# Attention and token mixer on one Trainium2 core: sixteen weight transfers move from SyncE's queue to ScalarE's

## Chip, cores and metric

The kernel runs on one core of a Trainium2 chip. The time is the device time of one execution in microseconds (us), given as the median of several runs. A profiled execution has a time of its own; its span, from the first to the last instruction, is a little shorter. The engines are PE (matmul; PEld is its weight load), DVE (VectorE), ACT (ScalarE), POOL (GpSimd) and SP (SyncE, which here only issues transfers).

## What is computed

The reference is block-causal attention over 8 batches, 8 heads, 576 positions and a head size of 64, followed by a low-rank token mixer and a feed-forward layer with a residual:

```python
scores = scale * np.matmul(q, k.transpose(0, 1, 3, 2))
scores = np.where(block_i >= block_j, scores, -1000000000.0)
attn = softmax(scores)
x = np.matmul(attn, v)          # heads joined: (8, 576, 512)
h = x.transpose(0, 2, 1) @ U @ V
u = x + h.transpose(0, 2, 1)
out = u + np.maximum(u @ w_ch1, 0.0) @ w_ch2    # 512 -> 2048 -> 512
```

q, k and v are 32-bit floats; U, V, w_ch1 and w_ch2 are 64-bit floats.

## The kernel before

**Work.** There are 64 heads, done one after the other. A head's scores, maxima, exponentials, sums, normalised rows, transposes and products with v come from `softmax`, `normalise`, `transpose` and `apply_v`. Heads 0 to 11 multiply q and k as plain 32-bit floats straight out of the buffer `raw`, of which there are two, so that head h uses the buffer of head h-2; `split_qk` (L881) fetches them (L886) and scales k on ACT (L902). After every second head `mix` (L1121) applies the token mixer to that pair of heads; after eight heads a batch's input of the feed-forward layer is complete.

**Feed-forward.** `ffn_chunk` (L431) takes 288 tokens and the first half (1024 of 2048) of the hidden units: L465 multiplies with w_ch1, L488 with w_ch2. Each operand is split into a high and a low part, and three products are added up. The two chunks of batch 0 run in two turns, the first with four of the eight blocks of 128 hidden units, the second with the others. The second half of the hidden units follows at the end, in `block_products` (L659). The feed-forward matmuls of the first half have a late rank (1e6 and up) on PE: they fill the holes that the heads leave.

**Weights of the first half.** `load_w1` and `load_w2` bring them in sixteen transfers of 128 rows x 512 doubles (512 KB): four of w_ch1 (ranks 3000 to 4500), four of w_ch2 (6100 to 7600), four of w_ch1 (9000 to 12000) and four of w_ch2 (13000 to 16000). Each goes through `split64` (L316): a fetch into `st`, one of two staging buffers; ACT takes the absolute value of the upper words (L353); DVE builds 32-bit floats from the two words in four passes (L331, L332, L337, L345); ACT writes the high part (L360), and POOL the rest (L361). `st` is free again after L345. The second half's sixteen transfers (`whole` set) use the same two buffers from about 660 us on. U and V go through `split64` first, at the start.

**Order.** Nothing is scheduled at run time. Every step is a task of the class `Plan` (L138) with an engine, an estimated duration, a rank (the smaller, the earlier), the buffers it reads and writes, and `after`, a further time until its result counts as there (transfers: `DL`, 3000 ns). `issue` (L165) runs a model of the engines: whenever one is free in the model, the ready task with the smallest rank is written out on it. The instruction streams that result are fixed, and on the chip each engine works through its own in that order, waiting for semaphores. A head h has ranks of about 1000h; its fetch of q and k has 1000(h-1) - 900. In the model a transfer of the weights keeps SP busy for max(630, 2.85 x 512) = 1459 ns.

**SP's queue before.** All transfers are issued by SP: q and k (L886), v (L925), the mixer's results to DRAM (L1173, L1178) and back (L440), the weights (L372, L387), the outputs (L499).

Of the kernel before, what the change touches and what calls it, by code (L numbers as in the profile page):

```python
# [16 lines left out]
P = 128  # L17
# [25 lines left out]
CW = 512  # L43
# [10 lines left out]
NEAR, DL = 130, 3000  # L54
# [83 lines left out]
class Plan:  # L138
# [8 lines left out]
    def add(self, engine, ns, prio, fn, reads=(), writes=(), hold=(), after=0, port=False):  # L147

        n = len(self.tasks)
        deps = set()  # L150
        for b in reads:
            deps.update(b.writers)
            b.readers.append(n)
        for b in hold:
            deps.update(b.readers, b.writers)
        for b in writes:
            deps.update(b.readers, b.writers)
            b.writers, b.readers = [n], []
        deps.discard(n)
        slots = {b for b in (*reads, *writes) if b.pool is not None}  # L160
        for b in slots:
            b.users += 1
        self.tasks.append((engine, ns, prio, fn, deps, after, slots, port or engine == "POOL"))
# [76 lines left out]
def _act(n, sbuf=False):  # L240
    return (93 if sbuf else 52) + 0.833 * n


def _dve(n):
    return 69 + 1.042 * n
# [9 lines left out]
def attention_then_mixer(  # L255
# [10 lines left out]
    nc = tc.nc  # L266
# [8 lines left out]
    add = plan.add  # L275

    def f32(ap):
        return ap.bitcast(F32)
# [29 lines left out]
    def take(r, name):  # L308
        n = used[name] = used.get(name, -1) + 1
        return r[n % len(r)]  # L310
# [2 lines left out]
    st_r = ring(fp, 2, [P, CW, 2], I32, "st")  # L313
    z_r = ring(fp, 2, [P, 2 * T], I32, "z")

    def split64(fetches, shape, hi, lo, dst, prio, gate=(), part=slice(None), whole=None):  # L316

        n = 1
        for x in shape[1:]:
            n *= x  # L320
        rows = shape[0]
        st, zt = take(st_r, "st"), take(z_r, "z")
        s, z = st[:rows, :n, :], zt[:rows, :n]
        low, upp = s[:, :, 0], s[:, :, 1]

        def fetch():
            for f in fetches:
                f(s)

        def shift():  # L330
            nc.vector.tensor_scalar(out=f32(z), in0=f32(z), scalar1=MOST, scalar2=LEAST, op0=ALU.min, op1=ALU.max)  # L331
            nc.vector.tensor_scalar(  # L332
                out=z, in0=z, scalar1=3, scalar2=0x3FFFFFFF, op0=ALU.logical_shift_left, op1=ALU.bitwise_and
            )

        def put_upper():
            nc.vector.scalar_tensor_tensor(  # L337
                out=z, in0=upp, scalar=-(1 << 30), in1=z, op0=ALU.bitwise_and, op1=ALU.bitwise_or
            )

        def put_lower():
            o, l, x = z, low, z
            if whole:
                o, l, x = whole().bitcast(I32), *(a.rearrange("p (a b) -> p a b", a=2) for a in (low, z))
            nc.vector.scalar_tensor_tensor(  # L345
                out=o, in0=l, scalar=29, in1=x, op0=ALU.logical_shift_right, op1=ALU.bitwise_or
            )

        zf = f32(z)
        if len(shape) > 2:  # L350
            zf = zf.rearrange("p (a b) -> p a b", a=shape[1])
        add("SP", max(630 * len(fetches), 2.85 * n), prio, fetch, gate, [st], after=DL)
        add("ACT", _act(n, True), prio, lambda: nc.scalar.activation(f32(z), f32(upp), AF.Abs), [st], [zt])  # L353
        add("DVE", 260 + 1.05 * n, prio, shift, [st, zt], [zt], port=True)
        add("DVE", _dve(n), prio, put_upper, [st, zt], [zt], port=True)
        if whole:
            add("DVE", _dve(n), prio, put_lower, [st, zt], dst if isinstance(dst, list) else [dst], port=True)
            return
        add("DVE", _dve(n), prio, put_lower, [st, zt], [zt], port=True)
        add("ACT", _act(n, True), prio, lambda: nc.scalar.copy(hi(), zf), [zt], [dst])  # L360
        add("POOL", 60 + 2.3 * n, prio, lambda: nc.gpsimd.tensor_sub(lo(), zf[part], f32(hi()[part])), [zt, dst], [dst])  # L361

    def load_w1(w, half, bufs, prio, parts=(0, 1), gate=(), whole=None):

        n = 0
        for o in parts:
            for k in range(KC):
                a = 2 * (half * HF + o * CW)
                at = (slice(None), k, slice(o * CW, (o + 1) * CW))
                src = w1[k * P : (k + 1) * P, a : a + 2 * CW]  # L370
                split64(
                    [lambda s, src=src: nc.sync.dma_start(out=s, in_=src.rearrange("p (n t) -> p n t", t=2))], [P, CW],  # L372
                    lambda at=at: w()["w1h"][at], lambda at=at: w()["w1l"][at],
                    bufs[o][k // 2] if whole else bufs["w1"][o][k], prio(n), gate,
                    whole=whole and (lambda o=o, k=k: whole()[:, o, k // 2, k % 2 * CW : (k % 2 + 1) * CW].rearrange(
                        "p (a b) -> p a b", a=2
                    )),
                )
                n += 1

    def load_w2(w, half, bufs, prio, gate=(), whole=None, ks=range(FC)):

        for k in ks:
            r = (half * FC + k) * P
            src = w2[r : r + P, :]
            split64(
                [lambda s, src=src: nc.sync.dma_start(out=s, in_=src.rearrange("p (n t) -> p n t", t=2))], [P, CW],  # L387
                lambda k=k: w()["w2h"][:, k, :], lambda k=k: w()["w2l"][:, k, :],
                [bufs[a][k // FH] for a in range(2)] if whole else bufs["w2"][k], prio(k), gate,
                whole=whole and (lambda k=k: whole()[:, :, k // FH, k % FH * 256 : (k % FH + 1) * 256]),  # L390
            )

    def weight_bufs():
# [109 lines left out]
    def block_products():  # L503
# [60 lines left out]

        s1 = {x: (at("w1h", n), at("w1l", n), after(end), after(end)) for n, (x, _) in enumerate(STAGES1)}
        load_w1(None, 1, whole, lambda n: L, whole=lambda: second()["whole"])
        weights(s1)

# [8 lines left out]
        for n, x in enumerate(("a11", "a12", "a22", "s2", "s3", "s1", "s4")):  # L577
            (hi, h), (lo, l) = place(2 * n), place(2 * n + 1)
            s2[x] = (hi, lo, h, l)
        load_w2(None, 1, whole, lambda k: L, whole=lambda: second()["whole"])  # L580
        weights(s2)

# [245 lines left out]
    for r in raw_r:  # L828
# [3 lines left out]
        for x, fill in ((qi, 1.0), (ki, NEG)):  # L832
            nc.gpsimd.affine_select(
                out=x[:, :, 1, :], in_=x[:, :, 1, :], pattern=[[-1, 4], [0, 64]], compare_op=ALU.not_equal,
# [13 lines left out]
    def mixing_weights(prio):  # L848


        def fetch_u(t):
# [3 lines left out]
            )  # L855

        split64(
            [fetch_u], [P, 4, R], lambda: ust[:, 0:4, 0:R], lambda: ust[:, 0:4, R : 2 * R], ust.parts[0], prio
        )
# [326 lines left out]
    mixing_weights(MP)  # L1186
    wab = weight_bufs()
    load_w1(lambda: wa, 0, wab, lambda n: WP0 + WP1 * n, (0,))
    for h in range(NH):
        pr = 1000.0 * h  # L1190
        if h + 1 < NH:
            split_qk(h + 1, max(pr - LA, 1.0))
        for g, tiles in ((1, (4, 3)), (0, (2, 1, 0))):
            for x in ((4,), (3,)) if g else ((2,), (1, 0)):
                softmax(h, x, pr + 10)
            normalise(h, tiles, pr + 10)
        for g in (1, 0):
            for part in range(2):
                transpose(h, g, part, pr + 20 + 10 * (1 - g))
            apply_v(h, g, pr + 30)  # L1200
        if h + 1 < NH:
            split_v(h + 1, pr + 1000)
        if h % 2 == 1:
            mix(h // 2, pr + 40)
        if h == min(WH, NH - 1):
            gate = Buf()
            gate.writers = [len(plan.tasks) - 1]
            load_w2(lambda: wa, 0, wab, lambda n: WPB + WP1 * n, [gate], ks=range(FH))
            load_w1(lambda: wa, 0, wab, lambda n: WP2 + WP3 * n, (1,), [gate])
            load_w2(lambda: wa, 0, wab, lambda n: WP4 + WP3 * (n - FH), [gate], ks=range(FH, FC))  # L1210
# [59 lines left out]
```

## Time and profile before

| | us |
|---|---|
| median of 3 runs | 1182.55 (1182.36 to 1183.16) |
| profiled execution | 1182.37 |
| its span | 1180.6 |
| PE busy | 1164.1 |
| DVE busy | 936.2 |
| ACT busy | 774.9 |
| POOL busy | 451.2 |
| first feed-forward matmul (L465) starts at | 99.95 |

An engine is busy while an instruction of it runs; waits, branches and the issuing of transfers do not count. Matmuls are pipelined, so a busy PE is not PE at its peak. The granted clock of PE is 1.00 throughout. In a row of a timeline stand the start, the length, the engine and line, the operation, what it writes and reads, and the count, with the idle time before it and what ended that in brackets. In a row of waits stand who waited, for whom, the total in us, how often, and the longest. "SPq" is SP's queue of transfers.

### The profile page before, as it was taken

To read this page: it belongs to the slowest core of one execution; us is meant where nothing else is said; L and a number is where in the kernel's file an instruction comes from. 1 tells how busy PE (TensorE), PEld (TensorE's weight loads), DVE (VectorE), ACT (ScalarE), POOL (GpSimd) and SP (SyncE) were. 2 spreads that over 40 slices of the span, in tenths; PEclk is the share of its full clock that TensorE was granted. 3 is DMA by queue.
4 is the path that set the end of the run, shared out by engine and by line. 5 is a ranking of instruction groups with operands and counts; after the bars stand their busy time and mean duration, and the time that the engine had idled before them with its cause. 6 is when DMAs were issued, how large, how long until landed. Compare 5 with 4: busy or idle time off the path is not lost.

```text
span 1180.6 us, 25204 instructions
## 1 busy us (share of the span) xinstructions
PE 1164.1 (99%) x8988; PEld 1131.4 (96%) x8988; DVE 936.2 (79%) x2009; ACT 774.9 (66%) x1924; POOL 451.2 (38%) x582
## 2 busy tenths in 40 slices
PE   9989999999999999999999999999999999999998
PEld 7778999999999999999999999999999999999998
DVE  6898887877887877777877587327989889889887
ACT  7888888989888888898887342114544444444443
POOL 5556876676757666766674122110000000000000
PEclk9999999999999999999999999999999999999999
DMA  4445565433433433443331434211132132132121
GB/s 142 141 153 154 160 177 140 116 115 108 114 112 110 123 105 111 114 117 110 112 94 52 142 113 145 66 52 50 61 122 71 51 121 70 53 121 62 60 81 41
DMA packets 75884, 122.69 MB, mean 104 GB/s; under 512 B 8944, under 2 KB 52976, under 8 KB 75760
## 3 DMA queue, kind: packets, MB, share of 16 engines
q1 hardware_dynamic: 75760, 121.09, 34.8%
q8 instruction: 71, 1.16, 0.4%
q14 instruction: 53, 0.43, 0.1%
HBM read 76.23 MB, written 29.49 MB: 90 GB/s over the span
## 4 chain that ended last, share of the span: by engine, by line
PE 81%; DVE 8%; ACT 7%; issue 2%; DMA 1%; SPq 0%; POOL 0%; ACTq 0%; DVEq 0%; POOLq 0%
PE bb L659 30%; PE bf L465 11%; PE bf L488 10%; PE ba L1050 7%; PE ba L1109 6%; PE bg L488 4%; PE bg L465 4%; ACT p L991 3%; DVE mx L980 2%; PE ba L967 2%; PE ba L966 2%; PE ba L1134 1%; PE bw L966 1%; PE ba L1148 1%; DVE pl L1069 1%
## 5 line engine op out<-in xcount | busy, mean ns | idle before, releaser
L1017 POOL TENSOR_SCALAR p<-p,rv 128x192 f32<-128x192 f32 (+4 forms) x320 | 171.8, 551 | 156.8 <-DVE rv L1008 85.2
L659 PE MATMUL bb<-hh,w1l 128*128 128x288 f32 x704 | 170.1, 295 | 0.0
L659 PE MATMUL bb<-hh,w1h 128*128 128x288 f32 x704 | 169.4, 295 | 0.0
L1069 DVE TENSOR_TENSOR pl<-ba,ph 128x512 fp32r<-128x512 f32 x216 | 113.7, 550 | 17.9 <-ACT ph L1027 15.7
L991 ACT ACTIVATE p<-ba,mx 128x448 f32<-128x448 f32 (+2 forms) x248 | 114.8, 466 | 16.4 <-DVE mx L980 12.8
L1050 PE MATMUL ba<-ident,p 128*128 128x128 f32 x768 | 122.8, 275 | 2.7 <-POOL p L1017 1.5
L659 PE MATMUL bb<-hl,w1h 128*128 128x288 f32 x576 | 123.0, 295 | 0.1
L659 PEld LDWEIGHTS bb<-hh,w1l 128*128 128x128 f32 x704 | 122.9, 190 | 0.0
L659 PEld LDWEIGHTS bb<-hh,w1h 128*128 128x128 f32 x704 | 121.9, 188 | 0.0
L488 PE MATMUL bf<-hh,w2h 128*128 128x288 f32 x384 | 118.8, 309 | 0.9 <-DVE hl L473 0.9
L488 PE MATMUL bf<-hl,w2h 128*128 128x288 f32 x384 | 113.5, 295 | 0.0
L488 PE MATMUL bf<-hh,w2l 128*128 128x288 f32 x384 | 112.7, 294 | 0.0
L447 POOL TENSOR_TENSOR ul<-ur,uh 128x288 fp32r<-128x288 f32 x72 | 61.5, 880 | 127.2 <-PE bf L465 80.9
L613 ACT CAST hh<-hb 128x576 fp32r<-128x576 f32 x98 | 65.9, 672 | 60.6 <-PE bb L659 59.3
L1027 ACT CAST ph<-ba 128x512 fp32r<-128x512 f32 x216 | 98.8, 491 | 9.1 <-PE ba L1050 7.8
L980 DVE TENSOR_REDUCE mx<-ba 128x1 f32<-128x448 f32 (+3 forms) x248 | 95.1, 406 | 10.1 <-PE ba L967 7.5
L1050 PEld LDWEIGHTS ba<-ident,p 128*128 128x128 f32 x768 | 89.9, 141 | 8.3 <-POOL p L1017 3.4
L659 PEld LDWEIGHTS bb<-hl,w1h 128*128 128x128 f32 x576 | 91.9, 188 | 0.4 <-DVE hl L614 0.4
L1109 PE MATMUL ba<-ph,vs 128*128 128x256 f32 (+3 forms) x432 | 89.9, 262 | 0.0
L465 PE MATMUL bf<-uh,w1l 128*128 128x288 f32 x392 | 82.1, 305 | 0.0
L913 POOL TENSOR_TENSOR k<-raw,k 64x576 fp32r<-64x576 f32 x52 | 75.1, 1444 | 2.1 <-POOL p L1017 0.5
L912 POOL TENSOR_TENSOR q<-raw,q 64x576 fp32r<-64x576 f32 x52 | 74.0, 1422 | 4.5 <-issue 2.1
(173 smaller groups left out, 3357.7 us busy)
## 6 DMA issues: line engine op xcount, KB each, us to landing
raw<-in_qk_dram SPq DMA_DIRECT2D x63, 288.0 KB, 3.9
st<-in_w_dram SPq DMA_DIRECT2D x32, 512.0 KB, 3.7
o_d<-ot SPq DMA_DIRECT2D x72, 144.0 KB, 1.8
vr<-in_v_dram SPq DMA_DIRECT2D x32, 320.0 KB, 3.7
ur<-u_d SPq DMA_DIRECT2D x64, 144.0 KB, 2.4
whole<-o_d SPq DMA_DIRECT2D x32, 288.0 KB, 3.1
out_dram<-whole SPq DMA_DIRECT2D x31, 288.0 KB, 2.2
ur<-u_d SPq DMA_DIRECT2D x30, 288.0 KB, 3.3
```

Source lines behind the costliest of these rows:

```text
L465: nc.tensor.matmul(ps[:, :T], w()[wn][:, k, fs], m[k].ap, start=(i == 0), stop=(i == len(ops) - 1))
L488: nc.tensor.matmul(ps[:, :T], w()[wn][:, f, ms], hs[f][x].ap, start=(i == 0), stop=(i == len(ops) - 1))
L659: nc.tensor.matmul(bank[:, i, :T], x()[:, w(k)], p.ap[:, k, :], start=first and n == 0, stop=last and n == len(ops) - 1)
L912: add("POOL", 1380, pr, lambda: nc.gpsimd.tensor_sub(q1[top], raw[top, 0:S], f32(q2[top])), [raw, q2], [q1])
L913: add("POOL", 1380, pr, lambda: nc.gpsimd.tensor_sub(k2[top], raw[top, S : 2 * S], f32(k1[top])), [raw, k1], [k2])
L980: lambda i=i, at=at: nc.vector.tensor_reduce(out=mx[: P if i else 64, i : i + 1], in_=view(i, at), op=ALU.max, axis=AX.XY if wide else AX. ...
L991: nc.scalar.activation(out.rearrange("p (j k) -> p j k", j=2) if wide else out, view(i, at), AF.Exp, bias=mx[:rows, i : i + 1], accum_out= ...
L1017: lambda x=x, rows=rows, i=i: nc.gpsimd.tensor_scalar(out=x, in0=x, scalar1=rv[:rows, i : i + 1], scalar2=1.0, op0=ALU.mult, op1=ALU.mult),
L1027: add("ACT", _act(n), pr, lambda: nc.scalar.copy(out(), inp()), reads, writes)
L1050: nc.tensor.transpose(out=bank[:, a : a + P], in_=pt_r[i][h % PB[i]][:, j * P : (j + 1) * P], identity=perm.ap)
L1069: "DVE", _dve(m), pr, lambda: nc.vector.tensor_sub(pl[:, low], bank[:, :m], f32(ph[:, low])), [bank, bh], [bl]
L1109: nc.tensor.matmul(bank[0 : c.stop, a:n], vs[:, j, c], x[:, _at(g, j)], start=(i == 0), stop=(i == len(ops) - 1))
```

## The change

`split64` gets an argument `queue`. For the first half's weights (`whole` not set) `load_w1` and `load_w2` now start the transfer with `nc.scalar` in place of `nc.sync`, and the task belongs to ACT, with 450 ns and a landing 1400 ns later than `DL`. The second half's transfers, U, V and all others stay with SP. No other line is touched; since the model of `Plan` sees other durations, the order of tasks on all engines is worked out anew.

```diff
-    def split64(fetches, shape, hi, lo, dst, prio, gate=(), part=slice(None), whole=None):
+    def split64(fetches, shape, hi, lo, dst, prio, gate=(), part=slice(None), whole=None, queue="SP"):
...
-        add("SP", max(630 * len(fetches), 2.85 * n), prio, fetch, gate, [st], after=DL)
+        if queue == "ACT":
+            add("ACT", 450, prio, fetch, gate, [st], after=DL + 1400)
+        else:
+            add("SP", max(630 * len(fetches), 2.85 * n), prio, fetch, gate, [st], after=DL)
...
     def load_w1(w, half, bufs, prio, parts=(0, 1), gate=(), whole=None):
 
-        n = 0
+        n, queue, start = 0, *(("SP", nc.sync) if whole else ("ACT", nc.scalar))
...
-                    [lambda s, src=src: nc.sync.dma_start(out=s, in_=src.rearrange("p (n t) -> p n t", t=2))], [P, CW],
+                    [lambda s, src=src: start.dma_start(out=s, in_=src.rearrange("p (n t) -> p n t", t=2))], [P, CW],
...
     def load_w2(w, half, bufs, prio, gate=(), whole=None, ks=range(FC)):
 
+        queue, start = ("SP", nc.sync) if whole else ("ACT", nc.scalar)
```

`load_w2` starts its transfer with `start.dma_start` in the same way, and both hand `queue=queue` to `split64`.

More of the change, by code (lines that the diff above doesn't have):

```diff
@@ L377, in load_w1 @@
                     )),
+                    queue=queue,
                 )
@@ L386, in load_w2 @@
             split64(
-                [lambda s, src=src: nc.sync.dma_start(out=s, in_=src.rearrange("p (n t) -> p n t", t=2))], [P, CW],
+                [lambda s, src=src: start.dma_start(out=s, in_=src.rearrange("p (n t) -> p n t", t=2))], [P, CW],
                 lambda k=k: w()["w2h"][:, k, :], lambda k=k: w()["w2l"][:, k, :],
@@ L390, in load_w2 @@
                 whole=whole and (lambda k=k: whole()[:, :, k // FH, k % FH * 256 : (k % FH + 1) * 256]),
+                queue=queue,
             )
```

## Prediction

> **What bounds the kernel now.** I read the page first, then the busy time by stretches, then what the matmul engine (PE) waited for, and last the rows around the sixteen transfers themselves.
>
> ```profile
> span 1180.6 us, 25204 instructions
> ...
> PE 1164.1 (99%) x8988; PEld 1131.4 (96%) x8988; DVE 936.2 (79%) x2009; ACT 774.9 (66%) x1924; POOL 451.2 (38%) x582
> ```
>
> PE is busy for 1164.1 of 1180.6 us. The change touches no matmul, so what it can win lies in the 16.5 us in which PE is idle, and in what hides in "busy" because matmuls wait for each other in the pipeline. The stretches (busy us and count of PE, of its weight loads, of DVE, ACT and POOL, then clock, DMA share and GB/s) say where the idle time lies:
>
> ```profile
> 0.00:80.00 80.00, 72.97 (x420) 59.85 (x421) 65.24 (x174) 64.81 (x180) 43.08 (x67) 1.00 0.46 143
> 80.00:160.00 80.00, 76.26 (x573) 69.80 (x572) 70.64 (x168) 67.26 (x185) 58.43 (x68) 1.00 0.59 168
> 160.00:480.00 320.00, 318.52 (x2632) 310.34 (x2631) 255.66 (x683) 281.50 (x794) 219.03 (x281) 1.00 0.41 116
> ```
>
> 7.0 + 3.7 = 10.8 us of the 16.5 us lie before 160 us; the next 320 us have 1.5 us. The weight loads on PE tell the same: 59.9 of 80 us at first, 310 of 320 later. So PE is loosely filled only until feed-forward matmuls, which can fill every hole, are there. Before that, the attention heads run as fast as their chain over PE, DVE, ACT and POOL allows, with ACT busy for 64.8 + 67.3 = 132 of 160 us (83%) and DVE for 136 (85%). The transfers that the change moves lie in just this part. What ended PE's waits before 160 us (total us, times, longest):
>
> ```profile
> PE bw L962 <- ACT raw L902: 2.3, 2, 1.2
> PE ba L1050 <- POOL p L1017: 1.5, 2, 0.8
> ...
> PE ba L1050 <- ACT p L991: 0.9, 2, 0.6
> ```
>
> ACT alone ends 3.2 us in these two rows. An ACT that falls behind is therefore felt by PE at this place, though not one for one.
>
> **What SP gives up.** Sixteen issues leave SP. Each is short, and SP stands waiting for the staging buffer before most of them (first duration ns min/median/max of the issue, then total wait us, times, longest):
>
> ```profile
> L372 SPq DMA_DIRECT2D st<-in_w_dram x16: 327/333/524, 17.7 to 685.5; - x16
> L387 SPq DMA_DIRECT2D st<-in_w_dram x16: 327/333/576, 41.0 to 735.2; - x16
> ```
> ```profile
> SPq L372 <- DVE z L345: 22.9, 8, 5.5
> SPq L387 <- DVE z L345: 21.1, 6, 6.6
> ```
>
> SP loses 16 x 0.333 = 5.3 us of issuing and up to 44.0 us of waiting. That would be a gain if something urgent were queued behind. Urgent on SP are the fetches of q and k for the head after next, which need the last score matmul that reads the buffer:
>
> ```profile
> 41.97 0.66 PE L962 MATMUL ba<-raw 128*128 128x192 f32 x4
> ...
> 44.75 1.30 PE L962 MATMUL ba<-raw 128*128 128x320 f32 x6
> ```
> ```profile
> 42.66 0.47 SPq L886 DMA_DIRECT2D raw<-in_qk_dram  x1
> ...
> 46.11 0.47 SPq L886 DMA_DIRECT2D raw<-in_qk_dram  x1
> ```
>
> The score matmuls end at 41.97 + 0.66 = 42.63 and 44.75 + 1.30 = 46.05 us, the fetches start at 42.66 and 46.11 us: 0.03 and 0.06 us later. They are bound by PE's release of the buffer, not by SP. I take 0 for SP's relief; at the outside it is worth these 0.06 us a fetch, some 0.7 us for the twelve heads whose scores read that buffer.
>
> The Trainium skill, "DMA: Bandwidth & Descriptors", section "Issuing engines are not separate DMA queues", says that issuing from several engines saves only the sequencer's issue time. The two lags agree that this time is not what anyone waits for here, so by that rule too SP's part is 0.
>
> **What a second queue may give.** One place shows a fetch that was late in landing. These rows are from SP's timeline, from the chain that ended last (start, us), and from ACT's and PE's timelines (idle before, in brackets):
>
> ```profile
> 41.01 0.33 SPq L387 DMA_DIRECT2D st<-in_w_dram  x1
> 41.39 0.90 SPq L1173 DMA_DIRECT2D u_d<-ur  x2
> ```
> ```profile
> 42.66 6.10 DMA raw<-in_qk_dram
> ```
> ```profile
> 48.78 0.68 ACT L902 ACTIVATE raw<-raw 64x576 f32<-64x576 f32 x1 [1.51 <-DMA raw<-in_qk_dram]
> ```
> ```profile
> 49.52 1.24 PE L962 MATMUL bw<-raw 128*128 128x288 f32 x4 [1.19 <-ACT raw L902]
> ```
>
> The fetch at 42.66 us came behind a weight transfer and two stores in one queue and took 6.10 us; ACT waited 1.51 us for it and PE 1.19 us. With the weight transfer in ACT's queue the fetch has only the stores ahead of it, but the same 512 KB go over the same DMA engines at about the same time. Bounds: 0 and -1.19 us. I take the middle, -0.6 us.
>
> The same page of the Trainium skill, section "Queues, rings and completion order", says that each DMA engine takes the queue rows in turn, packet by packet. By it the fetch would no longer stand behind the whole weight transfer, the full 1.19 us would be won, and the sum below would be 0.6 us lower; one queue is all that this trace has, so no row tests it.
>
> **What ACT takes on.** (1) The issues: 16 x 0.333 = 5.3 us if every one stops ACT; with the longest issue seen on SP it is 16 x 0.576 = 9.2 us; 0 if ACT's engine is still computing while its sequencer issues. The transfer's buffer is freed by the same DVE pass (L345) that frees the load's cast on ACT (L360). The cast has the smaller priority number, so the planner puts it first and the issue of the load after next behind it. The rows of DVE and of ACT there:
>
> ```profile
> 40.27 0.67 DVE L345 SCALAR_TENSOR_TENSOR z<-st,z 128x512 int32<-128x512 int32 x1
> ```
> ```profile
> 41.50 0.62 ACT L360 CAST w1h<-z 128x512 fp32r<-128x512 f32 x1
> 42.02 0.43 ACT L445 CAST uh<-ur 128x288 fp32r<-128x288 f32 x1
> ```
>
> The pass ends at 40.94 us. SP issued at 41.01 us; ACT would do it about at its cast, 41.5 to 42.1 us. A cast of 0.62 us is longer than an issue of 0.33 us, so most of it hides behind the cast, and what I charge is the overlap that is lost: the next instruction starts at 42.02 us, 0.10 us before the cast's end at 42.12 us. That is 16 x 0.10 = 1.6 us of ACT, of which I let a good third reach PE, +0.6 us. The bounds are 0 and the 9.2 us.
>
> (2) The wait for the buffer, behind which exponentials, copies and casts of the heads are queued, and so DVE, POOL and PE. The nearest rows are ACT's own waits for the same pass, before 160 us:
>
> ```profile
> ACT w1h L360 <- DVE z L345: 1.2, 2, 1.0
> ...
> ACT w2h L360 <- DVE z L345: 0.4, 1, 0.4
> ```
>
> ACT comes too early for that pass three times in sixteen, for 1.6 us in all, and that is paid already. An issue that stands behind the cast finds the pass done. I take 0; the other bound is the second rival.
>
> (3) The transfers start later, by 0.5 to 1.1 us in the example. Here is when weights are ready (POOL's last step of a load) and when PE first reads them:
>
> ```profile
> 50.06 1.26 POOL L361 TENSOR_TENSOR w1l<-z,w1h 128x512 fp32r<-128x512 f32 x1 [0.94 <-ACT w1h L360]
> ```
> ```profile
> 99.95 0.77 PE L465 MATMUL bf<-uh,w1h 128*128 128x288 f32 x4
> ```
> ```profile
> 158.62 1.28 POOL L361 TENSOR_TENSOR w2l<-z,w2h 128x512 fp32r<-128x512 f32 x1 [3.17 <-ACT w2h L360]
> ```
> ```profile
> 166.97 0.38 PE L488 MATMUL bf<-hh,w2h 128*128 128x288 f32 x1
> ```
>
> The first four are there at 51.3 us and used at 99.95 us; the sixteenth is there at 159.9 us, and the second turn that needs it starts at 166.97 us. 7.1 us of slack cover a delay of one or two; beyond 7.1 us each one would be PE's. I take 0.
>
> **The order.** The planner charges SP 1459 ns a transfer and a landing 3000 ns later; the change charges ACT 450 ns and 4400 ns. So the loads land 0.4 us later in its model and every later choice on every engine is taken anew. I see no reason for a sign and take 0, with 2.4 us to either side: the three rows of PE's waits above are six gaps with a sum of 4.7 us, 0.8 us each, so the 10.8 us are some fourteen such gaps; a new order closes some and opens others, and 2.4 us are three of them.
>
> **The sum.** Profiled execution 1182.37 us (its span of 1180.6 us and 1.8 us around it), 0.2 us below the median of 1182.55 us. 1182.37 + 0 (SP) - 0.6 (second queue) + 0.6 (issues) + 0 (waits) + 0 (later weights) + 0 (order) = 1182.4 us. Measurement tells about 0.2%, 2.4 us, from no change.
>
> **Rivals.** *The loads sink behind the heads (faster).* On SP a transfer went out as soon as its buffer was free; on ACT it must win by priority against the heads' work, which has the smaller numbers in most cases. If one or two loads slip past 100 us, DVE is relieved of their passes while the first eight heads, which the first feed-forward matmul waits for, are under way (total us, mean ns, before 160 us):
>
> ```profile
> L345 DVE SCALAR_TENSOR_TENSOR z<-st,z 128x512 int32<-128x512 int32 (+3 forms) x20 | 15.2, 762 | 0.0
> ...
> L331 DVE TENSOR_SCALAR z<-z 128x512 f32<-128x512 f32 (+3 forms) x20 | 13.6, 679 | 2.0 <-ACT z L353 1.8
> ```
>
> A load is four such passes, about 4 x 0.7 = 2.8 us of DVE at 85%. For it speaks that DVE is the busiest engine beside PE there; against it, that the planner already gives these passes the lower rank on DVE. If one load slips, the feed-forward starts up to 2.8 us sooner, with the second queue's 0.6 us about 1179.2 us. Chance 0.28.
>
> *ACT stalls at the issue (slower).* If the planner puts an issue where ACT comes to it well before the pass is done, ACT stops with all that is queued. SP's fourteen waits have a mean of 44.0 / 14 = 3.1 us. Two of these on ACT are 6.3 us; with half of that on PE, +3.1 us, and the time is 1185.5 us. It decides from two such stalls on; one, +1.6 us, is not told from no change. The cast's 1.6 us speak against it. Chance 0.18. To this side I add 0.04 for weights that come more than 7.1 us later.
>
> *The full issue cost.* If each issue stops ACT for its 0.333 us, 5.3 us of ACT cost at half about +2.7 us where I charged 0.6, so 1184.4 us: still within 2.4 us of the median, and part of my middle case. The Trainium skill, "Perfetto Trace Analysis", section "Sequencer Loop", says that engine instructions are pushed into a queue while control instructions run in the sequencer, which is the reading that makes this term small; only a trace with an issue on ACT can show it.
>
> **How the numbers follow.** The middle case has 0.50, and gives "within 0.2%"; faster has 0.28; slower 0.18 + 0.04 = 0.22. The range reaches to the faster rival's 1179.2 us and to the slower rival's 1185.5 us; what lies beyond is a part of each, together about 0.2.
>
> **What would show it.** Right: sixteen issues on ACT, each near 0.33 us and close behind a cast of the load before last; no ACT wait for L345 above 1 us; the first feed-forward matmul at 100 us, give or take 2; the q and k fetch of the seventh head landing in about 4 to 5 us; PE idle before 160 us of 9 to 13 us. Wrong: an issue that takes far longer than 0.33 us on ACT, waits of 3 us ahead of it, or a first feed-forward matmul that moved by more than 2.4 us.

## The result, and the profile after

The kernel became slower. Before: 1182.45 us (1181.61 to 1183.16). After: 1192.76 us (1192.20 to 1193.95). The ratio is 1.0089, with a 95% interval of 1.0071 to 1.0106, so 10.3 us or 0.9%. I had forecast no change (1182.4 us, up to 1185.5). The profiled execution of after took 1192.39 us. From L352 on, lines of after are 3 to 6 higher than those of before (L353 is L356, L372 is L375, L387 is L392, L465 is L471, L1050 is L1056); L331 to L345 are the same.

The page of after, span and engines:

```profile
span 1190.6 us, 25140 instructions
...
PE 1167.0 (98%) x8988; PEld 1134.8 (95%) x8988; DVE 939.7 (79%) x2009; ACT 777.8 (65%) x1924; POOL 454.2 (38%) x582
```

The span grew by 10.0 us. PE's busy time grew by only 2.9 us, its idle time by 7.1 us. The same three stretches of after as were shown of before (busy us and count of PE, PEld, DVE, ACT, POOL, then clock, DMA share and GB/s):

```profile
0.00:80.00 80.00, 74.12 (x416) 60.96 (x417) 59.24 (x169) 62.63 (x174) 40.38 (x66) 0.98 0.44 131
80.00:160.00 80.00, 72.55 (x527) 65.19 (x526) 69.16 (x158) 64.95 (x175) 57.13 (x66) 1.00 0.53 162
160.00:480.00 320.00, 314.26 (x2591) 307.19 (x2590) 250.86 (x662) 272.64 (x765) 214.05 (x271) 0.99 0.41 116
```

Look at the counts rather than at the busy time. By 160 us PE has started 416 + 527 = 943 matmuls, where before it had started 993; by 480 us 3534, where before it was 3625. So after is 50 matmuls behind at 160 us and 91 at 480 us. In the 360 us that follow, before does 2831 matmuls, 0.127 us each:

```profile
480.00:840.00 360.00, 358.96 (x2831) 354.26 (x2830) 242.83 (x548) 206.16 (x530) 130.68 (x167) 1.00 0.33 99
```

91 x 0.127 = 11.6 us, which is the 10.0 us of the span within what a count of mixed matmuls can say. Note also that in the first 80 us PE looks busier than before (74.1 for 73.0 us) with fewer matmuls done: "busy" hides the loss, the count shows it. A part of that is the granted clock (0.98 in this row): where it fell, at 44.81 us, six matmuls of 128x320 in L1099 take 2.23 us, and the same six in before take 1.20 us.

The sixteen issues themselves look as forecast. From the view of the staging buffer `st` in after (duration ns min/median/max, first and last start us), and a stretch of ACT's timeline:

```profile
L375 ACTq DMA_DIRECT2D st<-in_w_dram x8: 334/334/381, 20.8 to 108.3; - x8
L392 ACTq DMA_DIRECT2D st<-in_w_dram x8: 334/334/356, 49.4 to 147.5; - x8
```
```profile
22.05 0.44 ACT L363 CAST v<-z 96x288 fp32r<-96x288 f32 x1
22.06 0.33 ACTq L375 DMA_DIRECT2D st<-in_w_dram  x1
22.39 0.73 ACT L997 ACTIVATE p<-bw,mx 128x576 f32<-128x576 f32 x1
```

The issue (22.06 to 22.39 us) runs under the cast, and the exponential follows at once. But the loads come much later. DVE's pass L345, which frees `st`, for the twelfth of the sixteen loads, in before and in after:

```profile
102.91 0.66 DVE L345 SCALAR_TENSOR_TENSOR z<-st,z 128x512 int32<-128x512 int32 x1
```
```profile
124.61 0.69 DVE L345 SCALAR_TENSOR_TENSOR z<-st,z 128x512 int32<-128x512 int32 x1
```

That is 21.7 us later. The first feed-forward matmul of after starts at 103.65 us, 3.7 us later than before:

```profile
103.65 0.77 PE L471 MATMUL bf<-uh,w1h 128*128 128x288 f32 x4
```

Four stretches of 5 us in after show where PE stood, with the same columns:

```profile
40.00:45.00 5.00, 3.23 (x13) 2.30 (x14) 4.16 (x11) 4.23 (x13) 3.31 (x6) 0.86 0.71 186
45.00:50.00 5.00, 5.00 (x26) 3.97 (x25) 4.13 (x9) 3.61 (x9) 1.89 (x3) 0.80 0.19 66
175.00:180.00 5.00, 3.15 (x23) 2.52 (x21) 4.92 (x9) 4.95 (x12) 4.18 (x5) 1.00 0.49 148
180.00:185.00 5.00, 4.53 (x24) 4.56 (x25) 3.07 (x10) 1.00 (x4) 2.73 (x3) 0.66 0.23 62
```

Two of these are holes (3.2 of 5 us busy). DVE and ACT are at 4.9 of 5 us in the second, so PE seems to stand there for them. The row that ends it, with its wait of 2.20 us, is a product of the token mixer:

```profile
180.47 0.58 PE L1169 MATMUL ba<-v,t 96*128 96x288 f32 x1 [2.20 <-DVE rv L1013]
```

The DVE step that it names, at 180.25 us, runs behind two long passes of a load:

```profile
176.63 1.55 DVE L331 TENSOR_SCALAR z<-z 128x512 f32<-128x512 f32 x1
178.22 1.51 DVE L332 TENSOR_SCALAR z<-z 128x512 int32<-128x512 int32 x1
```

This load is not one of the sixteen, whose last L345 ends at 163.70 us. It is the first of the second half, which SP fetched already at 155.84 us; the "about 660 us" given ahead of the prediction holds for its last pass, not for its transfer. In before the same two passes took 0.68 and 0.53 us. Why they last so long here was not followed.

In or just behind each hole the granted clock falls (0.86 and 0.80; 0.66). 5 x (0.14 + 0.20) = 1.7 and 5 x 0.34 = 1.7 us are lost there by this estimate, 3.4 us of the 10 if PE bounds both.

### The profile page after: what moved, and what is told of

Same layout as the page of the kernel before. It is cut to its first block, busy times and chain, and to the rows that moved or that the text cites. A ratio compares the mean times of both kernels' runs of the same rounds, so it can differ in the third digit from the quotient of the medians.

```text
span 1190.6 us, 25140 instructions
## 1 busy us (share of the span) xinstructions
PE 1167.0 (98%) x8988; PEld 1134.8 (95%) x8988; DVE 939.7 (79%) x2009; ACT 777.8 (65%) x1924; POOL 454.2 (38%) x582
## 4 chain that ended last, share of the span: by engine, by line
PE 51%; ACT 1%; DVE 1%; issue 0%; ACTq 0%; DVEq 0%
PE bb L665 29%; PE bf L494 5%; PE bf L471 4%; PE bg L494 4%; PE bg L471 4%; PE ba L1056 1%; PE ba L1115 1%; ACT p L997 0%; PE ba L973 0%; PE ba L972 0%; PE ba L1140 0%; PE ba L1154 0%; PE bw L972 0%; PE bw L973 0%; DVE hl L620 0%
## 5 line engine op out<-in xcount | busy, mean ns | idle before, releaser
L1023 POOL TENSOR_SCALAR p<-p,rv 128x576 f32<-128x576 f32 (+4 forms) x320 | 173.0, 555 | 136.7 <-DVE rv L1014 62.4
L997 ACT ACTIVATE p<-ba,mx 128x448 f32<-128x448 f32 (+3 forms) x248 | 114.9, 466 | 16.4 <-DVE mx L986 11.9
L1056 PE MATMUL ba<-ident,p 128*128 128x128 f32 x768 | 123.2, 275 | 2.3 <-POOL p L1023 1.0
L494 PE MATMUL bf<-hh,w2h 128*128 128x288 f32 x392 | 121.7, 310 | 0.6 <-DVE ot L500 0.5
L494 PE MATMUL bf<-hl,w2h 128*128 128x288 f32 x392 | 116.3, 297 | 0.0
L494 PE MATMUL bf<-hh,w2l 128*128 128x288 f32 x392 | 115.7, 295 | 0.0
L1033 ACT CAST ph<-ba 128x512 fp32r<-128x512 f32 x216 | 100.4, 490 | 13.9 <-PE ba L1056 8.3
L1056 PEld LDWEIGHTS ba<-ident,p 128*128 128x128 f32 x768 | 90.3, 141 | 6.3 <-issue 3.4
L471 PE MATMUL bf<-uh,w1l 128*128 128x288 f32 x404 | 82.6, 302 | 0.0
L494 PEld LDWEIGHTS bf<-hh,w2h 128*128 128x128 f32 x392 | 74.5, 190 | 1.4 <-DVE ot L500 0.9
```

The lines of the kernel that those rows point to most:

```text
L471: nc.tensor.matmul(ps[:, :T], w()[wn][:, k, fs], m[k].ap, start=(i == 0), stop=(i == len(ops) - 1))
L494: nc.tensor.matmul(ps[:, :T], w()[wn][:, f, ms], hs[f][x].ap, start=(i == 0), stop=(i == len(ops) - 1))
L997: nc.scalar.activation(out.rearrange("p (j k) -> p j k", j=2) if wide else out, view(i, at), AF.Exp, bias=mx[:rows, i : i + 1], accum_out= ...
L1023: lambda x=x, rows=rows, i=i: nc.gpsimd.tensor_scalar(out=x, in0=x, scalar1=rv[:rows, i : i + 1], scalar2=1.0, op0=ALU.mult, op1=ALU.mult),
L1033: add("ACT", _act(n), pr, lambda: nc.scalar.copy(out(), inp()), reads, writes)
L1056: nc.tensor.transpose(out=bank[:, a : a + P], in_=pt_r[i][h % PB[i]][:, j * P : (j + 1) * P], identity=perm.ap)
```

## The experiments

Four explanations were set against each other. They are the letters in the expectations:

- **A, the rank.** On SP an issue goes out when its buffer is free. On ACT it must win by rank against the heads' work, so the loads slide behind the heads and come too late.
- **B, the order.** The planner's output changed, and before's order is a good one among many; any other set of numbers, with no ACT in it, would cost too.
- **C, the issue.** Issuing on ACT holds ACT up on the chip.
- **M, the model.** The loss is a hole that the planner's own model already shows: its end goes from 1141.4 us (before) to 1145.6 us (after).

Ratios are to the kernel before on the same chip, with 95% intervals; "model" is the end by the planner's model.

### The order and the issuing engine, apart

The order of the instructions is fixed when the kernel is written out, so the two halves of the change can be separated cleanly. First, before's order on all engines, with the sixteen transfers issued by ACT at the planned place:

```diff
-  [lambda s, src=src: nc.sync.dma_start(...)]
+  [lambda s, src=src: (nc.sync if whole else nc.scalar).dma_start(...)]
```

> The order of the kernel before on PE, DVE, ACT and POOL, unchanged; only the sixteen issues are taken out of SP's stream and put into ACT's, at the place that the model's time gives them. Theory B (the order that the planner writes out decides): 1181 to 1185 us. Theory C (the issue on ACT costs, by its own length and by waiting for the buffer in ACT's stream): at 16 x 0.34 us and the waits, 1186 to 1192 us. Theory A (loads that start late): the issues stand where they stood, so 1181 to 1186 us.

Second, after's order with SP as the issuer (the planner still takes the tasks for ACT's):

```diff
-  n, queue, start = 0, *(("SP", nc.sync) if whole else ("ACT", nc.scalar))
+  n, queue, start = 0, *(("SP", nc.sync) if whole else ("ACT", nc.sync))
...
-  queue, start = ("SP", nc.sync) if whole else ("ACT", nc.scalar)
+  queue, start = ("SP", nc.sync) if whole else ("ACT", nc.sync)
```

> The order of the changed kernel on PE, DVE, ACT and POOL, unchanged; only the sixteen issues are taken out of ACT's stream and put into SP's. Theory B: as slow as the changed kernel, 1189 to 1194 us. Theory C: the loss goes with the issues, 1181 to 1185 us. Theory A: SP starts a transfer as soon as the buffer is free, so the data are there earlier, but ACT's absolute value stands at its late place, so still 1187 us or more.

Measured: before's order issued by ACT takes 1183.81 us, ratio 1.0008 (0.9995 to 1.0020). After's order issued by SP takes 1190.42 us, ratio 1.0071 (1.0052 to 1.0089). The stretches, first of before's order issued by ACT, then of after's order issued by SP:

```profile
0.00:80.00 80.00, 72.41 (x413) 59.18 (x414) 63.62 (x170) 64.37 (x178) 43.10 (x67) 0.98 0.49 143
80.00:160.00 80.00, 75.81 (x564) 69.11 (x563) 70.25 (x168) 66.27 (x183) 57.26 (x68) 1.00 0.58 161
160.00:480.00 320.00, 318.50 (x2630) 310.64 (x2629) 255.99 (x684) 281.96 (x794) 219.79 (x281) 1.00 0.43 117
```
```profile
0.00:80.00 80.00, 73.40 (x417) 59.92 (x417) 59.67 (x170) 62.71 (x174) 40.50 (x66) 0.98 0.46 132
80.00:160.00 80.00, 73.34 (x535) 66.38 (x535) 70.66 (x158) 65.32 (x176) 58.13 (x66) 1.00 0.57 165
160.00:480.00 320.00, 314.27 (x2601) 307.13 (x2600) 251.64 (x667) 274.74 (x773) 215.30 (x275) 1.00 0.42 115
```

The second kernel has after's fingerprint with not one issue on ACT: DVE 59.7 us in the first 80, 952 matmuls by 160 us and 3553 by 480 us, that is 72 short of before's 3625, or 72 x 0.127 = 9.1 us. The first has before's: 3607 matmuls, 18 short, 2.3 us. The slide of the twelfth load is in the order too, here in after's order issued by SP:

```profile
124.38 0.69 DVE L345 SCALAR_TENSOR_TENSOR z<-st,z 128x512 int32<-128x512 int32 x1
```

So the order carries 1190.42 - 1182.61 = 7.8 us, some 8 of the 10.3 us. What the issue on ACT adds is 0.0008 x 1183 = 0.9 us by the one pair and (1.0089 - 1.0071) x 1183 = 2.1 us by the other; the interval of the one holds no change, and those of the other pair overlap. C is at most a small part. Nor is the granted clock the main part: the profiled execution of after's order issued by SP has one fall of its own (0.92 and 0.74 from 10 to 20 us), but another of its four runs kept a clock of 1.000 and took 1190.13 us.

### The rank

After, with its sixteen tasks put ahead of all other work of ACT:

```diff
-            add("ACT", 450, prio, fetch, gate, [st], after=DL + 1400)
+            add("ACT", 450, -1.0, fetch, gate, [st], after=DL + 1400)
```

> The changed kernel, but the sixteen issues on ACT get the rank -1, ahead of the heads' work, so that in the model ACT issues as soon as the staging buffer is free. Theory A (the loads slide: an issue on ACT waits for its turn behind the heads' work, each load starts later, and the loads' passes on DVE fall into the stretch behind 100 us): the sixteenth L345 ends near 158 us as before, not near 164, and the time comes back to 1182 to 1185 us. Theory B (any new order of the planner may cost this much, whoever issues): anything from 1178 to 1194 us, without a link to when the loads end. Theory C (ACT itself is held up on the chip by issuing): sixteen issues stay on ACT, now with more waiting for the buffer, so 1190 us or more.

Measured: 1184.63 us, 1.0015 (1.0006 to 1.0025), model 1143.6. Most of the loss is gone with ACT still issuing. The twelfth load and the first feed-forward matmul of this kernel:

```profile
106.86 1.00 DVE L345 SCALAR_TENSOR_TENSOR z<-st,z 128x512 int32<-128x512 int32 x1
```
```profile
100.43 0.77 PE L471 MATMUL bf<-uh,w1h 128*128 128x288 f32 x4
```

The loads are back (106.9 against 124.6 us), and so is the feed-forward (100.4 against 103.7 us). Two more kernels with this rank have other landing times (`after=DL + 500` and `DL + 900`), to see whether the good time belongs to the rank or to one lucky order:

> Sixteen issues on ACT with rank -1 and a model landing of 3500 ns in place of 4400. The planner's own model of the order ends 0.9 us earlier than for the kernel before (1140.5 against 1141.4 us in its own time). Theory B (a new order costs some us on the chip, whatever its model says): 1183 to 1190 us. Theory M (the loss is the hole that the model itself shows: 4.2 us later for the changed kernel): 1180 to 1183 us.

> The same with a model landing of 3900 ns; the model ends 1.1 us later than for the kernel before. Theory B: 1183 to 1190 us, and no nearer to the 3500 ns version than to others. Theory M: 1183 to 1185 us.

Measured: 1188.15 us, 1.0042 (1.0029 to 1.0054), model 1140.5; and 1186.37 us, 1.0021 (1.0012 to 1.0031), model 1142.5. And after with its old rank and only the landing put back (`after=DL`):

> The changed kernel with the old rank and a model landing of 3000 ns in place of 4400. The model ends 5.2 us later than for the kernel before, 1.0 us later than for the changed one. Theory B: 1184 to 1195 us. Theory M: 1187 to 1194 us, no faster than the changed kernel. If the 4400 ns were the cause of the loss: 1182 to 1185 us.

Measured: 1196.95 us, 1.0113 (1.0096 to 1.0130), model 1146.6: the slowest of all. So the 1400 ns do not make the loss. Much of this one is the granted clock, 0.990 to 0.993 in its four runs: in the profiled execution it is 0.83, 0.86 and 0.80 in the three stretches of 20 us from 140 to 200 us, by estimate 20 x (0.17 + 0.14 + 0.20) = 10.2 of the 14.1 us if PE bounds there. With all sixteen issues on ACT, the two orders with the heads' ranks cost 0.89 and 1.13%; with the first rank the three cost 0.15 to 0.42%. This speaks for A, but does not show it: each of the five is an order of its own, the first rank leaves a loss that differs from number to number, and it doesn't always keep the loads early. With 3500 ns the twelfth load is late with the first rank, too:

```profile
118.02 1.38 DVE L345 SCALAR_TENSOR_TENSOR z<-st,z 128x512 int32<-128x512 int32 x1
```

### Other numbers, with SP throughout

These kernels have no issue on ACT and no task of ACT's; only the numbers that the planner is given change. First SP with after's numbers (`queue` is handed on as in after, and the start is `nc.sync`):

```diff
-        add("SP", max(630 * len(fetches), 2.85 * n), prio, fetch, gate, [st], after=DL)
+        if queue == "ACT":
+            add("SP", 450, prio, fetch, gate, [st], after=DL + 1400)
+        else:
+            add("SP", max(630 * len(fetches), 2.85 * n), prio, fetch, gate, [st], after=DL)
```

> SP issues again, but the planner is given ACT's numbers for it, 450 ns and a landing 4400 ns later. Theory A: SP starts a transfer as soon as its buffer is free, so the loads end as before and the time is 1180 to 1185 us. Theory B: the model's numbers are those of the change, so the order is new, and the time may be anywhere from 1178 to 1194 us. Theory C: no issue on ACT, 1181 to 1184 us.

Then before, with the landing of the sixteen transfers 400 ns later or earlier, or with 330 ns for the issue and the landing 400 ns later:

```diff
-  add("SP", max(630 * len(fetches), 2.85 * n), ..., after=DL)
+  add("SP", max(630 * len(fetches), 2.85 * n), ..., after=DL + (400 if n == CW and not whole else 0))
```

> The kernel before, all on SP; only the model's landing time of these sixteen transfers is 3400 ns in place of 3000. That is the shift of the model's landing that the change brings, without any change of queue. Theory B: a new order on all engines, and a time that is off by several us in some direction, more likely slower, 1180 to 1192 us. Theories A and C: no issue on ACT and no waiting for a turn, 1181 to 1184 us.

> The same with 2600 ns. Theory B: again a new order, and a time off by several us, 1180 to 1192 us, with no link to the sign of the 400 ns. Theories A and C: 1181 to 1184 us.

> All on SP, and the planner is told what the chip shows for these sixteen: 330 ns of SP and a landing 3400 ns later. The model ends 1.8 us earlier than for the kernel before. Theory B: 1183 to 1190 us, for it is a new order too. Theory M: 1179 to 1182 us.

Last, two numbers that have nothing to do with the weights: the landing of q and k 200 ns later (`after=DL + 200`, L898), and POOL's normalise at 260 in place of 250 (L1016):

> The kernel before, the sixteen transfers as they were; only the model's landing time of the q and k fetches is 3200 ns in place of 3000. Theory B (any new order costs, since the order before is one of the better ones): slower by 0.1 to 0.6%, 1184 to 1190 us. If the losses belong to the weight transfers: 1181 to 1184 us.

> The kernel before; only the model's duration of the normalising step on POOL is 10 ns longer (260 + 0.85 w in place of 250 + 0.85 w). The planner's model ends 0.5 us earlier. Theory B: slower by 0.1 to 0.6%, 1184 to 1190 us. If the losses belong to the weight transfers: 1181 to 1184 us.

| kernel | time, us | ratio | interval | model, us |
|---|---|---|---|---|
| sp_with_act_numbers | 1190.36 | 1.0058 | 1.0041 to 1.0074 | 1141.0 |
| sp_landing_plus400 | 1185.50 | 1.0025 | 1.0013 to 1.0036 | 1141.0 |
| sp_landing_minus400 | 1187.77 | 1.0041 | 1.0025 to 1.0056 | 1142.9 |
| sp_cost330 | 1184.66 | 1.0016 | 1.0006 to 1.0025 | 1139.6 |
| other_raw_landing | 1183.58 | 1.0008 | 0.9998 to 1.0019 | 1143.7 |
| other_norm_cost | 1187.93 | 1.0033 | 1.0013 to 1.0052 | 1140.9 |

Not one is faster, and five of six are measurably slower, among them one that changes nothing but a normalise's estimate by 10 ns. A landing 400 ns later costs and one 400 ns earlier costs as well. This is B: before's numbers give an order that is among the good ones, and a draw of another order costs 0.1 to 0.6%. In sp_with_act_numbers the loads sink little: their L345 starts 2.6 us later than in before on the mean of the sixteen, against 11.5 us in after, and the twelfth is in its place. Still 6.9 us are lost:

```profile
103.24 0.66 DVE L345 SCALAR_TENSOR_TENSOR z<-st,z 128x512 int32<-128x512 int32 x1
```

So a loss nearly as large as that of after's order came with hardly a sinking load.

A part of these losses is the granted clock, and it is not the same part in each. Two stretches of other_norm_cost, whose seven runs all lie at 0.993 to 0.999:

```profile
60.00:80.00 20.00, 17.06 (x100) 14.18 (x100) 16.30 (x35) 13.69 (x38) 9.22 (x11) 0.91 0.41 122
80.00:100.00 20.00, 16.30 (x87) 12.80 (x86) 17.49 (x38) 16.10 (x45) 11.75 (x16) 0.91 0.46 141
```

By estimate 20 x (0.09 + 0.09) = 3.6 of its 4.7 us are lost there if PE bounds both. In the runs with a clock of 1.000 the kernel before takes 1182.3 us (median), sp_landing_plus400 1183.2 (two runs), other_raw_landing 1183.4, sp_cost330 1184.6 and sp_landing_minus400 1186.1 us (one run). So four of the orders cost 0.9 to 3.8 us without any fall of the clock, and again none is faster; the other two have no such run.

M falls as a guide: by the model sp_cost330 should have won 1.8 us and lost 1.8, other_norm_cost should have won 0.5 and lost 4.7, other_raw_landing should have lost 2.3 and shows 0.3. Of all these, only the two orders with the heads' ranks for all sixteen on ACT have a model end more than 4 us later (1145.6 and 1146.6), and they are the two slowest; there model and chip agree in sign, and the model shows less than half of the loss.

### Parts of the change

Only the first four transfers on ACT, and only the last twelve:

```diff
-  n, queue, start = 0, *(("SP", nc.sync) if whole else ("ACT", nc.scalar))
+  n, queue, start = 0, *(("SP", nc.sync) if whole or 0 not in parts else ("ACT", nc.scalar))
...
-  queue, start = ("SP", nc.sync) if whole else ("ACT", nc.scalar)
+  queue, start = "SP", nc.sync
```

For the last twelve the condition is `whole or 0 in parts`, and `load_w2` is as in after.

> Only the first four transfers (w_ch1, ranks 3000 to 4500) are issued by ACT, the other twelve by SP. Theory A: the first loads slide by 6 to 8 us as in the changed kernel and the rest catch up in part, so a part of the loss, 1183 to 1188 us. Theory B: no ordering, 1178 to 1194 us. Theory C: a quarter of the loss, about 1185 us.

> Only the last twelve transfers are issued by ACT, the first four by SP. Theory A: the first four loads run as before, the later ones slide; most of the loss, 1185 to 1192 us, with the sixteenth L345 ending behind 160 us. Theory B: 1178 to 1194 us. Theory C: three quarters of the loss, about 1190 us.

Measured: 1187.39 us, 1.0030 (1.0018 to 1.0042); and 1189.21 us, 1.0049 (1.0034 to 1.0065). Each part costs, but each is also a new order and lies within what new orders cost with SP alone. These two tell nothing apart, and I should not have expected them to.

### What an issue on ACT costs

Before's order, with each transfer as two of 64 rows, once on ACT (32 issues) and once on SP, to double the number of issues on ACT without a new order:

```diff
-  [lambda s, src=src: nc.sync.dma_start(out=s, ...)]
+  [lambda s, src=src, h=h: (nc.sync if whole else nc.scalar).dma_start(out=s[h], ...)
+      for h in ((slice(0, P),) if whole else (slice(0, 64), slice(64, P)))]
```

On SP the same halves are issued with `nc.sync` throughout.

> The same with the thirty-two issues on ACT, still in the order of the kernel before. Theory C: twice the cost of sixteen issues; if these cost 0.9 to 2 us, 2 to 4 us more than the run with halves on SP. Theory B: the order is the same, so within 2 us of it.

> The order of the kernel before on every engine; each of the sixteen transfers is issued as two of 64 rows, on SP. The control of the next run. All theories: 1181 to 1184 us.

Measured: on ACT 1191.85 us, 1.0069 (1.0054 to 1.0084); on SP 1184.17 us, 1.0007 (0.9996 to 1.0018). The halves cost nothing on SP and (1.0069 - 1.0007) x 1183 = 7.3 us on ACT, where single issues had cost 0.9. The cost is not linear in the number. ACT's timeline with the halves shows why; "x2" is two issues back to back:

```profile
43.01 0.67 ACT L353 ACTIVATE z<-st 128x512 f32<-128x512 f32 x1
43.57 1.12 ACTq L387 DMA_DIRECT2D st<-in_w_dram  x2
44.73 0.36 ACT L1027 COPY xt<-ba 64x256 f32<-64x256 f32 x1 [1.05 <-DVE ur L1168]
...
51.53 0.68 ACT L902 ACTIVATE raw<-raw 64x576 f32<-64x576 f32 x1 [0.62 <-DMA raw<-in_qk_dram]
51.53 1.19 ACTq L387 DMA_DIRECT2D st<-in_w_dram  x2
52.76 0.62 ACT L360 CAST w1h<-z 128x512 fp32r<-128x512 f32 x1 [0.55 <-issue]
```

The second pair starts together with an instruction of 0.68 us, takes 1.19 us, and ACT stands for 0.55 us. The first starts only when DVE has freed the buffer (L345 ends at 42.86 + 0.67 = 43.53 us), 0.11 us before the activation ends, and ACT stands for nearly all of its 1.12 us, 1.05 us. ACT's next instruction starts 0.04 us after each pair's end. The place of the first pair with single issues, in before's order issued by ACT, DVE's pass first:

```profile
42.27 0.67 DVE L345 SCALAR_TENSOR_TENSOR z<-st,z 128x512 int32<-128x512 int32 x1
```
```profile
42.42 0.67 ACT L353 ACTIVATE z<-st 128x512 f32<-128x512 f32 x1
42.98 0.34 ACTq L387 DMA_DIRECT2D st<-in_w_dram  x1
43.35 0.36 ACT L1027 COPY xt<-ba 64x256 f32<-64x256 f32 x1 [0.26 <-DVE ur L1168]
43.74 0.62 ACT L360 CAST w1h<-z 128x512 fp32r<-128x512 f32 x1
```

The gap of 0.26 us here carries the name of a DVE instruction, as did the 1.05 us above. It begins where the activation ends (43.09 us) and ends 0.03 us after the issue (43.32 us): the issue was the last to end, whatever the bracket says. It could not start sooner, since the buffer came free at 42.94 us: what ACT loses depends on when the release comes, too. Over the sixteen places ACT's gaps between the instruction before an issue and the next one behind it add up to 2.5 us with single issues and 11.9 us with halves (ACT's timelines up to 170 us). That PE pays for it shows in the count: 392 + 521 = 913 matmuls by 160 us with the halves on ACT, 80 short of before's 993, or 10.2 us; the span is 9.3 us longer (1189.9 us). Stretches of the halves on ACT:

```profile
0.00:80.00 80.00, 69.22 (x392) 55.30 (x393) 60.48 (x167) 60.96 (x170) 40.14 (x62) 1.00 0.50 132
80.00:160.00 80.00, 72.46 (x521) 65.15 (x520) 67.70 (x157) 64.42 (x174) 56.64 (x67) 1.00 0.58 153
```

No kernel here beats the kernel before.

## Why the prediction was wrong

**The step that failed** is the order: "I see no reason for a sign and take 0, with 2.4 us to either side". It measures +7.8 us (after's order issued by SP), three times the bound. Two things in that step were wrong. The first is the mean of zero: of the six orders with other numbers and SP as the only issuer, none is better than before's. A step that is planned anew here is a draw from such orders, at +0.1 to +0.6%, and not a coin. The second is the bound: I sized it by PE's named waits before 160 us, 4.7 us in six gaps. One of those three rows (L1050 for ACT's L991, 0.9 us) is of the whole execution and doesn't occur before 160 us, so 3.8 us in four gaps are left. By them three gaps are 2.9 us and not 2.4, and that is not what failed; ACT's rows there still add up to 4.8 us. The 10.0 us of the span are 13.3 - 10.8 = 2.5 us more idle PE before 160 us, 5.7 - 1.5 = 4.3 us more in the 320 us behind, where the row of before had so little that I looked no further, 2.9 us more "busy" PE, and 0.3 us elsewhere. Three quarters of the loss lie outside the gaps from which I took the bound.

**The rival "the loads sink behind the heads"** (0.28) had the mechanism right and the sign wrong. The loads did sink: the twelfth by 21.7 us. DVE was relieved as priced: its busy time in the first 80 us fell from 65.24 to 59.24 us, 6.0 us, about two loads at my 2.8 us. But the first feed-forward matmul came 3.7 us later, not 2.8 sooner. The heads didn't gain from the free DVE, and the loads' passes came back later, from 102 to 164 us; the hole at 175 us is not theirs. That the sinking is part of the cause is not shown. With the first rank the loss shrinks to 0.15 to 0.42%, which speaks for it; sp_with_act_numbers loses 0.58% with the loads close to their places, which speaks for the order alone. How much of the 7.8 us is the sinking itself, and how much the draw of any new order, stays open: no order was run in which the loads alone move. Where in the chain the heads lose was not followed to a single wait either.

**The rival "ACT stalls at the issue"** (0.18) had the sign right and the mechanism wrong. ACT's waits in after for the pass that frees the buffer, before 160 us:

```profile
ACT w1h L363 <- DVE z L345: 1.9, 4, 1.1
...
ACT w2h L363 <- DVE z L345: 1.5, 2, 0.8
```

These are casts; none of 3 us ahead of an issue, and after's order with SP in ACT's place keeps 7.8 of the 10.3 us. At the sixteen issues of after ACT's idle time adds up to 1.1 us. So the 0 for the wait for the buffer was right here, though only six of the sixteen issues stand right behind a cast, where I had expected all.

**SP's relief, 0**: not refuted. With before's order SP is rid of its sixteen issues and the time is 0.9 us higher, not lower; but this is the net of SP's relief, the second queue and the issues, for which I had summed 0.

**The second queue, -0.6 us**: right in size where it can be seen. PE waited 1.19 us for the scaled k of the seventh head; in before's order issued by ACT, with the fetch in another queue than the weights, it waits 0.50 us:

```profile
51.07 1.24 PE L962 MATMUL bw<-raw 128*128 128x288 f32 x4 [0.50 <-ACT raw L902]
```

That is 0.7 us less, and the fetch that it waits for took 5.37 us in place of 6.10, where I had written 4 to 5. The Trainium skill, "DMA: Bandwidth & Descriptors", section "Queues, rings and completion order", by which I had put the gain at the whole 1.19 us, goes the right way and is not borne out in full.

**The issues on ACT, +0.6 us**: of the right size, if the same 0.9 us of net, with an interval that holds zero, is theirs; with the second queue's 0.7 us it would be 1.6 us. Both lie near the lower end of my bounds of 0 to 9.2 us. The Trainium skill, "Perfetto Trace Analysis", section "Sequencer Loop", has the sequencer push engine instructions into a queue and start control instructions itself. The trace agrees for the issue of 0.33 us at 22.06 us of after, which runs under a cast of 0.44 us; at the two pairs above no more than that one instruction covered them.

**Later weights, 0 with 7.1 us of slack**: not refuted. In before's order issued by ACT the twelfth load is 2.1 us later than in before (104.99 for 102.91 us) and the ratio is 1.0008:

```profile
104.99 0.66 DVE L345 SCALAR_TENSOR_TENSOR z<-st,z 128x512 int32<-128x512 int32 x1
```

In after the delay, 21.7 us for this load, is far beyond that slack. I had priced delays by the length of an issue, not by a place in a queue of ranks. The rival's 1179.2 us, too, is 1182.55 - 2.8 - 0.6, taken from the median and without the issues; by the terms of the sum it is 1182.4 - 2.8 = 1179.6 us, and nothing hangs on it.

**What would show it**: the issues' length and the absence of long waits ahead of them came as I wrote, their place did not, and the longest wait for L345 is 1.1 us, just over my 1; the first feed-forward matmul moved by 3.7 us, more than the 2.4 us that I had named as the sign of being wrong; PE's idle time before 160 us, 13.3 us, lies just outside my 9 to 13.

## What to carry to other kernels

Where a static planner writes the order, an edit that changes a task's engine, cost or landing is two edits: price the order separately, by running the new order with the old operation and the old order with the new one, and expect a new order to cost when the old one was among the good ones. Compare the granted clocks as well, since an order can lose time by them. A task that is moved to a busy engine keeps its rank but not its place: what was prompt on an idle queue waits its turn behind whatever has the smaller rank, so ask which rank it needs there. Single issues on a computing engine were nearly free here, where they ran under the instruction before them; two in a row were not.

## What the runs showed of the hardware

One issue of 128 rows takes 0.33 us on ACT as on SP, and one of 64 rows takes longer, 0.47 us at the least:

```profile
L372 ACTq DMA_DIRECT2D st<-in_w_dram x16: 472/578/682, 18.3 to 94.8; - x16
L387 ACTq DMA_DIRECT2D st<-in_w_dram x16: 472/473/1027, 43.6 to 136.3; - x16
```

These are rows of the halves on ACT. So halving a transfer makes each issue longer by 0.14 us or more, and a pair at 1.12 to 1.19 us costs more than three single issues. Why was not looked into.

The granted clock can fall for a few us in a kernel whose PE is 98% busy: 0.66 of full speed at 180 to 185 us in after, behind 5 us with PE busy for 3.15. A hole alone doesn't decide it. After's order issued by SP has a deeper one and keeps its clock there:

```profile
175.00:180.00 5.00, 2.68 (x20) 2.24 (x19) 4.89 (x9) 4.05 (x9) 3.68 (x4) 1.00 0.51 148
180.00:185.00 5.00, 5.00 (x43) 5.00 (x42) 4.35 (x11) 2.24 (x9) 2.29 (x3) 1.00 0.56 163
```

Since that kernel is 7.8 us slower without this fall, and still takes 1190.13 us in the run with a clock of 1.000, the clock isn't the cause of the main loss; it may be the 2.1 us between it and after, for which the issues on ACT are the other candidate. That was not settled.
